# Sparse attention on two sequences in turns, with transfers that serve both, ahead of a routed expert layer

## The chip, the cores and the metric

The kernel runs on one core of a Trainium2 chip. The metric is the device time of one execution in microseconds (us); a kernel's time is the median of its runs. All arithmetic that matters here is float32.

## What is computed

The reference has two stages. The first is block-sparse attention over 4 sequences of 768 tokens, with 8 heads of 64 channels. A sequence has 24 blocks of 32 tokens. A query block sees its own block, its two neighbours, the first and the last block, and three random blocks that the input `sampled_blocks` names; the first and the last query block see all keys. The second stage sends each token to one of 8 experts, by the cosine of its attention output with 8 embeddings, and puts it through that expert's two matrices.

```python
scores = scale * np.matmul(q, k.transpose(0, 1, 3, 2))
mask = np.abs(blk_i - blk_j) <= window
mask = mask | (blk_i == 0) | (blk_j == 0) | (blk_i == n_blocks - 1) | (blk_j == n_blocks - 1)
# ... and True for the three sampled blocks of each query block
attn = softmax(np.where(mask, scores, -1e9))
x = np.matmul(attn, v)                        # (4, 8, 768, 64) -> 3072 tokens of 512
...
expert_idx = argmax(cosine(x, expert_emb) / tau)
out[mask_e] = gate * (np.maximum(x[mask_e] @ w1[e], 0.0) @ w2[e])
```

## The kernel before, in words

**Steps.** A sequence is cut into 6 chunks of 128 queries, rotated by one block, so that chunk 0 holds the last block, the first block and blocks 1 and 2. The loop of `attention_fast` (L1272) makes one chunk per step, s = 0 to 23, and a last step 24 that finishes chunk 23: sequence 0's six chunks, then sequence 1's, and so on. Step s scores chunk s and weighs the values of chunk s-1. In the order of the program a step does:

- `fetch_all` (L434): the loads of this step and the gathers for chunk s+1, all issued from the SyncE queue (SP);
- `score_near` (L510, tile `ac`) and `score_far` (L541, `dps`): scores with near keys and with gathered keys, each followed by an exponential on ScalarE;
- `gather_k` (L484): copies of key blocks for chunk s+1, by VectorE and GpSimd;
- `weigh_near` part 0, `turn_x` of chunk s-2 (L677), one `turn_k` (L456), `weigh_far` (L627): PE's products with V;
- `near_v` (L445): four GpSimd copies of neighbour blocks of V into the gather tile of chunk s+1;
- `turn_q` of chunk s+1 (L472), the logits of chunk s-2, `weigh_near` part 1, `normalize` (L645).

`manual_schedule` keeps the attention in this order on each engine; behind it a scheduler interleaves the experts.

**Queries that see all keys.** In the step that scores a sequence's chunk 0, `score_ends` (L561, tile `bps`) makes the scores of the first and last query block with all 768 keys, four head pairs into four tiles `pb`; the next step's `weigh_far` multiplies them with all six V tiles (L638). For that all of a sequence's K and V must be there at its first chunk.

**V.** `load_v` brings a whole sequence into one of two tiles `vst` (8 DMAs). `gather_v` (L424) fetches, for each of 4 query blocks and 3 random slots, a block of 32 tokens x 8 heads straight from DRAM into a gather tile `vg`, at an offset in a register: 12 DMAs of 64 KB per chunk (6 for chunk 0), into a ring of 3 tiles. `fetch_all` puts the step's other loads between them: K of the next sequence, Q of chunk s+3, V of the next sequence. A row of Q, K or V is 64 float32 values, 256 bytes, and each is a packet of its own.

**The start.** SP issues in order the K of sequence 0 (8 DMAs), the embeddings and tau (`load_experts`, L201), the V of sequence 0 (8), and then, once the offsets are known, the gathers. ScalarE's queue issues the Q of chunks 0 and 1. PE turns the four K pairs and makes `score_ends` between them. `build_experts` (L209) normalizes the embeddings, in pieces put between the first steps.

**Routing.** `after_sequence` (L1193) plans `route` (L740) of a whole sequence of 6 chunks over the steps behind it: a power on GpSimd, some ten small VectorE operations, the one-hot choice, running counts (`seen`, L773) on GpSimd, and x written to DRAM. After two sequences `dispatch_early` assigns tokens to 5 early expert tiles; two `fetch_rows` (L1037) and the first expert's weights (8 DMAs of 512 KB) follow from step 20 on. The last sequence's `route` runs between the first expert tiles (`last_route`, L1437), ahead of `rank` (L800).

**The experts.** 25 tiles of up to 128 tokens follow, some 14 us each: two matrix products per tile (L1126, L1139), with 4 MB of weights each.

Of the kernel before, what the change touches and what calls it, by code (L numbers as in the profile page):

```python
# [12 lines left out]
F32 = mybir.dt.float32  # L13
# [39 lines left out]
NCH = B * NC  # L53
DEN_LOW, DEN_HIGH = 0.1, 1e10
# [72 lines left out]
def build_tokens(k, shifted):  # L127
# [3 lines left out]
    nc.gpsimd.iota(tok, pattern=[[-S, B], [-P, NC]], base=N + BLK * shifted, channel_multiplier=-1)  # L131
    if shifted:
        first = tok.rearrange("p (b c) -> p b c", c=NC)[:, :, 0]
        nc.vector.tensor_scalar(out=first[0:BLK], in0=first[0:BLK], scalar1=-S, scalar2=None, op0=ALU.add)
# [245 lines left out]
def load_q(k, n):  # L380

    b, c = divmod(n, NC)
    k.raw["q", n] = t = k.ld.tile([P, H, D], F32, name="qraw", tag="qraw", bufs=3)
    src = k.q[b].rearrange("h s d -> s h d")
    return [(t[rows], src[lo:lo + rows.stop - rows.start]) for rows, lo in pieces(c)]


def load_k(k, g, pool=None):

    b, j = divmod(g, NPAIR)  # L390
    k.raw["k", g] = t = (pool or k.ld).tile([P, NC, 2, D], F32, name="kraw", tag="kraw", bufs=2 if pool else 3)
# [3 lines left out]
def load_v(k, b):  # L395

    v = k.vst[b % 2]
    src = k.v[b].rearrange("h s d -> s h d")
    parts = []
    parts.append((v[0:BLK, 0, :, 0:D], src[S - BLK:S]))  # L400
    parts.append((v[BLK:P, 0, :, 0:D], src[0:P - BLK]))
    for m in range(1, NC):
        parts.append((v[:, m, :, 0:D], src[P * m - BLK:P * (m + 1) - BLK]))
    return parts


def keep_ends(k, b):

    k.nc.gpsimd.tensor_copy(out=k.vg0[b % 2][D:P], in_=k.vst[b % 2][0:D, 0])
# [14 lines left out]
def gather_v(k, n):  # L424

    b, c = divmod(n, NC)
    k.vg[n] = t = k.vg_ring[n % len(k.vg_ring)]
    src = k.v[b].rearrange("h s d -> s h d")
    for s in range(NRAND):
        for g, shift in zip(blocks_of(c), shifts(k, mybir.EngineType.SP, s, c)):  # L430
            yield t[s * BLK:(s + 1) * BLK, g, :, 0:D], src[bass.ds(shift, BLK)]
# [13 lines left out]
def near_v(k, n):  # L445

    b, c = divmod(n, NC)
    for g in blocks_of(c):
        block = NG * c + g - 2 if g % 2 == 0 else NG * c + g
        if 0 < block < NB - 1:  # L450
            rows, m = home(block)
            k.nc.gpsimd.tensor_copy(out=k.vg[n][NRAND * BLK:P, g], in_=k.vst[b % 2][rows, m])  # L452


def turn_k(k, g):

    nc = k.nc
    b, j = divmod(g, NPAIR)
    raw = k.raw.pop(("k", g))
# [4 lines left out]
    copy(out=k.kt[b % 2][:, j].rearrange("p (w t) -> p w t", w=2), in_=ps[:, :, 0:3 * P])  # L464
    pairs = slice(j, j + 1) if b == 0 else slice(0, NPAIR)
    if j == pairs.stop - 1:
        for i, block in enumerate((NB - 1, 0)):
            nc.scalar.copy(out=k.ke[b % 2][:, pairs, i * BLK:(i + 1) * BLK],
                           in_=k.kt[b % 2][:, pairs, block * BLK:(block + 1) * BLK])


def turn_q(k, n):  # L472

    raw = k.raw.pop(("q", n))
    ps = ring(k, "xg_ps", 0, 1, k.eps, [P, ND, P])
    for j in range(NPAIR):
        k.nc.tensor.transpose(ps[:, j], raw[:, 2 * j:2 * j + 2, :].rearrange("p h d -> p (h d)"), k.ident)  # L477
# [6 lines left out]
def gather_k(k, n):  # L484

    nc = k.nc
    b, c = divmod(n, NC)
    kt = k.kt[b % 2]
# [21 lines left out]
def score_near(k, n):  # L510

    nc = k.nc
    b, c = divmod(n, NC)
    kt, qt = k.kt[b % 2], k.qt[n]
    ps = k.big.tile([P, 2, 512], F32, name="ac", tag="big")
    halves = (1,) if c == 0 else (0, 1)
    for j in range(NPAIR):
        for half in (None, *halves):
            r, lo = near_at(j, half)
            for h in range(2):  # L520
                rows = slice(D * h, D * (h + 1))
                if half is None:
                    cols = slice(D * halves[0], P)
                    keys = k.ke[b % 2][rows, j]
# [15 lines left out]
def score_far(k, n):  # L540

    nc = k.nc
    b, c = divmod(n, NC)
# [17 lines left out]
def score_ends(k, n, j):  # L561

    nc = k.nc
    b = n // NC
    kt, qt = k.kt[b % 2], k.qt[n]
    ps = k.big.tile([P, 2, 512], F32, name="bps", tag="big")
    for m in range(NC):
        for r in range(2):
            for h in range(2):
                rows = slice(D * h, D * (h + 1))  # L570
                lo = D * (2 * m + r) - BLK
                keys = k.ke[b % 2][rows, j] if m == 0 and r == 0 else kt[rows, j, lo:lo + D]
                nc.tensor.matmul(ps[D * r:D * (r + 1), h, D * m:D * (m + 1)], lhsT=keys, rhs=qt[rows, j, h, 0:D],  # L573
                                 start=True, stop=True)
    k.pb[j] = e = k.pb_pool.tile([P, 2, NC, D], F32, name=f"pb{j}", tag=f"pb{j}")
    nc.scalar.activation(e.rearrange("p h m t -> p h (m t)"), ps[:, :, 0:NC * D], ACT.Exp, scale=SCALE)

# [17 lines left out]
def weigh_near(k, n, turn):  # L595

    b, c = divmod(n, NC)
# [955 lines left out]
```

## Time and profile before

| | |
|---|---|
| median of 3 runs | 655.94 us (649.62 to 663.33) |
| the profiled execution: its time, its span | 656.3 us, 654.5 us |
| mean granted TensorE clock | 0.970 |
| PE, weight loads (PEld) busy | 609.0 us (93%), 476.1 us (73%) |
| VectorE (DVE), GpSimd (POOL), ScalarE (ACT) busy | 226.1, 235.2, 118.8 us |
| attention | from 0 to 287.5 us |
| expert tiles | from 277 us on; alone from 301 us on |

All times below that begin at 0 count from the start of the span. The profile is one execution, with the instructions of each engine, the DMA packets and the semaphores. The chain of waits follows the work that ended last back to the start: each piece is the instruction that ran, or the DMA that was waited for. The table of windows gives for chosen stretches the length, then each engine's busy time (with its instructions), PE's granted clock, the mean busy share of the 16 DMA engines, and the GB/s that they moved. SPq is SP's queue, where DMAs are issued; an issue that is long is not a transfer that is long.

### The profile page before, as it was taken

What the parts mean: (1) busy time and instruction counts of PE and PEld (TensorE: products, weight loads), DVE (VectorE), ACT (ScalarE), POOL (GpSimd) and SP (SyncE); (2) the same over time, 40 slices, a digit from 0 to 9 for tenths busy, and PEclk for the clock granted to TensorE, in tenths of its full rate; (3) what the DMA queues carried; (4) which work ended last, traced back from release to release, by engine and by line L of the source; (5) the groups of instructions that cost most, each with busy time, mean ns of one, the idle gap of its engine ahead of it and who ended that gap; (6) DMA issues with size and microseconds to landing.
All of it is one profiled execution on the core that took longest, in us unless ns stands there. A gap on an engine that the chain in (4) does not pass through costs nothing.

```text
span 654.5 us, 21692 instructions
## 1 busy us (share of the span) xinstructions
PE 609.0 (93%) x9016; PEld 476.1 (73%) x9016; DVE 226.1 (35%) x661; ACT 118.8 (18%) x265; POOL 235.2 (36%) x446
## 2 busy tenths in 40 slices
PE   7799899896989799797999999999999999999995
PEld 5598789886989699676776677774667756666773
DVE  6654436542656556127511121122112111211210
ACT  2424344343243324100000000000000000000000
POOL 1853252534163428002033334443333443333332
PEclk9999999899998989797999999999999999999999
DMA  9866666768576757999999989999899998999611
GB/s 189 165 150 146 145 150 137 160 141 212 131 160 140 193 125 190 198 322 397 368 406 394 393 338 307 340 349 340 310 401 402 403 375 307 416 388 404 265 49 33
DMA packets 189758, 170.80 MB, mean 261 GB/s; under 512 B 150152, under 2 KB 150280, under 8 KB 186834
## 3 DMA queue, kind: packets, MB, share of 16 engines
q1 hardware_dynamic: 182338, 155.36, 75.3%
q0 software_dynamic: 5216, 13.43, 6.0%
q8 instruction: 73, 1.20, 0.8%
q10 hardware_dynamic: 2096, 0.52, 0.4%
q14 instruction: 35, 0.29, 0.1%
HBM read 156.65 MB, written 12.90 MB: 259 GB/s over the span
## 4 chain that ended last, share of the span: by engine, by line
PE 83%; issue 4%; DMA 3%; POOL 2%; DVE 2%; SPq 2%; ACT 1%; POOLq 0%; DVEq 0%; ACTq 0%
PE hp L1126 26%; PE yp L1139 24%; PE av L586 11%; PE dps L551 5%; PE ac L529 3%; PE yp L693 3%; DMA vg<-in_v_dram 2%; PE hp L1171 2%; PE yp L1191 2%; PE xg_ps L682 2%; PE xg_ps L477 2%; PE bps L573 2%; SPq L440 1%; PE kps L462 1%; DMA vst<-in_v_dram 1%
## 5 line engine op out<-in xcount | busy, mean ns | idle before, releaser
L1126 PEld LDWEIGHTS hp<-xgt,w 128*128 128x128 f32 x1472 | 170.5, 195 | 10.2 <-issue 10.2
L1126 PE MATMUL hp<-xgt,w 128*128 128x128 f32 x1472 | 171.4, 278 | 0.0
L1139 PE MATMUL yp<-w,h 128*128 128x512 f32 x368 | 162.0, 593 | 0.0
L1139 PEld LDWEIGHTS yp<-w,h 128*128 128x128 f32 x368 | 68.2, 190 | 76.5 <-issue 76.2
L1050 POOL DMA_INDIRECT xg<-x_dram,quarter x88 | 88.5, 1006 | 30.1 <-issue 27.4
L1152 POOL DMA_INDIRECT out_dram<-y,slot_l x20 | 20.3, 1015 | 156.8 <-DVE y L1151 156.8
L494 POOL COPY kg<-kt 128x128 f32 x176 | 44.6, 297 | 65.4 <-issue 36.6
L1129 ACT ACTIVATE h<-hp 128x512 f32<-128x512 f32 x23 | 13.7, 597 | 290.8 <-PE hp L1126 290.8
L452 POOL COPY vg<-vst 32x520 f32<-32x520 f32 x80 | 49.7, 621 | 39.8 <-PE av L586 28.0
L1133 DVE TENSOR_SCALAR h<-hp 128x512 f32<-128x512 f32 x23 | 15.9, 691 | 134.8 <-PE hp L1126 134.8
L586 PE MATMUL av<-vst,pac 64*64 64x65 f32 x1056 | 49.1, 231 | 7.1 <-issue 6.2
L481 DVE COPY qt<-xg_ps 64x512 f32<-64x512 f32 x48 | 33.0, 688 | 57.8 <-PE xg_ps L477 57.1
L1151 DVE TENSOR_SCALAR y<-yp,gate 128x512 f32<-128x512 f32 x20 | 15.0, 751 | 102.3 <-PE yp L1139 90.1
L551 PE MATMUL dps<-qt,kg 128*64 128x64 f32 x1408 | 47.9, 226 | 2.0 <-issue 2.0
L551 PEld LDWEIGHTS dps<-qt,kg 128*64 128x64 f32 x1408 | 44.4, 141 | 3.9 <-issue 2.3
L586 PEld LDWEIGHTS av<-vst,pac 64*64 64x64 f32 x1056 | 40.8, 142 | 6.5 <-issue 3.6
L586 PE MATMUL av<-vg,pd 128*32 128x65 f32 x1408 | 31.4, 230 | 10.9 <-DMA vg<-in_v_dram 4.4
L586 PEld LDWEIGHTS av<-vg,pd 128*32 128x32 f32 x1408 | 25.4, 115 | 17.0 <-issue 9.8
L556 ACT ACTIVATE pd<-dps,bias 128x256 f32<-128x256 f32 x88 | 34.6, 473 | 6.8 <-PE dps L551 6.2
L684 DVE COPY xt<-xg_ps 128x512 f32<-128x512 f32 x24 | 16.5, 688 | 46.3 <-PE xg_ps L682 46.3
L529 PE MATMUL ac<-qt,ke 64*64 64x128 f32 (+1 forms) x384 | 28.8, 276 | 1.3 <-DVE qt L481 1.3
L586 PE MATMUL av<-vg,pac 64*64 64x65 f32 x352 | 29.4, 240 | 0.5 <-issue 0.5
(229 smaller groups left out, 629.7 us busy)
## 6 DMA issues: line engine op xcount, KB each, us to landing
w<-in_moe_w_dram SPq DMA_DIRECT2D x52, 2048.0 KB, 17.1
vg<-in_v_dram SPq DMA_DIRECT2D x264, 64.0 KB, 3.2
kraw<-in_k_dram SPq DMA_DIRECT2D x32, 192.0 KB, 3.4
vst<-in_v_dram SPq DMA_DIRECT2D x20, 256.0 KB, 5.3
qraw<-in_q_dram SPq DMA_DIRECT2D x19, 256.0 KB, 4.3
w<-in_moe_w_dram SPq DMA_DIRECT2D x8, 512.0 KB, 5.8
x_dram<-x SPq DMA_DIRECT2D x4, 774.0 KB, 6.7
x_dram<-x SPq DMA_DIRECT2D x4, 516.0 KB, 3.4
```

Source lines behind the costliest of these rows:

```text
L452: k.nc.gpsimd.tensor_copy(out=k.vg[n][NRAND * BLK:P, g], in_=k.vst[b % 2][rows, m])
L481: k.nc.vector.tensor_copy(out=t[rows, :, h], in_=ps[rows])
L494: copy(out=t[:, :, g, s * BLK:(s + 1) * BLK], in_=kt[:, :, bass.ds(shift, BLK)])
L529: nc.tensor.matmul(ps[D * r:D * (r + 1), h, lo:lo + cols.stop - cols.start], lhsT=keys, rhs=qt[rows, j, h, cols], start=True, stop=True)
L551: nc.tensor.matmul(out[D * r:D * (r + 1), NG * j + g], lhsT=kg[:, j, g, D * r:D * (r + 1)], rhs=qt[:, j, :, cols], start=True, stop=True)
L556: nc.scalar.activation(e[:, :, g].rearrange("p j h t -> p j (h t)"), out.rearrange("p (j g) h t -> p j g (h t)", g=NG)[:, :, g], ACT.Exp, ...
L586: k.nc.tensor.matmul(av[lanes, h // NPAIR, h % NPAIR * P:h % NPAIR * P + D + 1], lhsT=lhsT, rhs=rhs, start=first[0], stop=last, skip_group ...
L693: k.nc.tensor.matmul(ps[:, 0:E], lhsT=xt[:, j], rhs=k.en[:, j, :], start=(j == 0), stop=(j == ND - 1))
L1050: k.nc.gpsimd.indirect_dma_start(out=x[:, g], out_offset=None, in_=quarters, in_offset=bass.IndirectOffsetOnAxis(ap=k.quarter[:, g, t:t + ...
L1126: nc.tensor.matmul(hp[:, f, :], lhsT=w1[:, d, (f0 + f) * P:(f0 + f + 1) * P], rhs=xt[:, d, :], start=(d == 0), stop=(d == ND - 1))
L1139: nc.tensor.matmul(yp, lhsT=h[:, f, :], rhs=w2[:, f, :], start=(f == 0), stop=(f == NF - 1))
L1152: k.scattered = nc.gpsimd.indirect_dma_start(out=k.out[:, :], out_offset=bass.IndirectOffsetOnAxis(ap=slot, axis=0), in_=y[:, :], in_offse ...
```

## The change

The steps now alternate between two sequences: step n is chunk c of sequence DUO*a + i, with i = n mod 2. Steps 0 to 11 are the chunks of sequences 0 and 1, steps 12 to 23 those of 2 and 3.

- One DMA brings Q rows, V rows or a random V block of both sequences: 16 rows of 256 bytes per token instead of 8. A gather is issued for a pair of steps, at the even one, behind `weigh_far` and `turn_q` of that step; the gather ring has 2 tiles of twice the size, the ring of Q tiles 2 of twice the size in place of 3.
- V lies in 7 tiles, one per chunk position, each for both sequences; the second pair's tile m takes the place of tile m-1. `near_v` copies both sequences in one copy, two of the four groups per step.
- K of sequences 2 and 3 is loaded and turned at listed steps (`loading`, `turning`); K of 0 and 1 is loaded at the start, and sequence 1's is turned in step 0.
- `score_ends` moves from the step that scores a chunk 0 to the next one, two head pairs at a time, through two `pb` tiles instead of four.
- `route` runs for 2 chunks, 12 times instead of 4; x goes out in one DMA (two for chunk 0) where a sequence took four. `rank` still runs per 6 chunks.
- `load_experts` stands behind the 16 K loads and the first V tile. `fetch_rows` of tile 1 moves from step 20 to the end of the attention.

```diff
+DUO = 2
+NS = NCH // DUO
+NV = NC + 1
...
+def place(n):
+
+    a, rest = divmod(n, DUO * NC)
+    c, i = divmod(rest, DUO)
+    return DUO * a + i, c, i
...
+def both(src, a):
+
+    return src[DUO * a:DUO * (a + 1)].rearrange("i h s d -> s (i h) d")
+
+
+def load_q(k, s):
+
+    a, c = divmod(s, NC)
+    k.raw["q", s] = t = k.ld.tile([P, DUO * H, D], F32, name="qraw", tag="qraw", bufs=2)
+    src = both(k.q, a)
...
+def gather_v(k, s):
+
+    a, c = divmod(s, NC)
+    k.vg[s] = t = k.vg_ring[s % len(k.vg_ring)]
+    src = both(k.v, a)
+    for r in range(NRAND):
+        for g, shift in zip(blocks_of(c), shifts(k, mybir.EngineType.SP, r, c)):
+            yield (t[r * BLK:(r + 1) * BLK, g].rearrange("p i h e -> p (i h) e")[:, :, 0:D], src[bass.ds(shift, BLK)])
...
+def near_v(k, s, some):
+
+    a, c = divmod(s, NC)
     for g in blocks_of(c):
         block = NG * c + g - 2 if g % 2 == 0 else NG * c + g
-        if 0 < block < NB - 1:
+        if g in some and 0 < block < NB - 1:
             rows, m = home(block)
-            k.nc.gpsimd.tensor_copy(out=k.vg[n][NRAND * BLK:P, g], in_=k.vst[b % 2][rows, m])
+            k.nc.gpsimd.tensor_copy(out=k.vg_ring[s % len(k.vg_ring)][NRAND * BLK:P, g], in_=vtile(k, a, m)[rows])
...
+    n.vg_ring = [n.gp.tile([P, NG, DUO, H, D + 1], F32, name=f"vg{i}", tag=f"vg{i}", bufs=1) for i in range(2)]
...
+    for s in range(2):
+        for to, src in load_q(n, s):
+            nc.scalar.dma_start(out=to, in_=src)
+    for g in range(2 * NPAIR):
+        fetch_all(n, None, load_k(n, g, n.setup if g < 5 else None))
+    fetch_all(n, None, load_v(n, 0, 0))
     load_experts(n)
-    fetch_all(n, None, load_v(n, 0))
...
+    fetch_all(n, 0, [])
+    for m in range(1, NC):
+        fetch_all(n, None, load_v(n, 0, m))
     turn_q(n, 0)
     for g in range(NPAIR):
         turn_k(n, g)
-        if g:
-            score_ends(n, 0, g - 1)
-    score_ends(n, 0, NPAIR - 1)
...
+    turning = {0: range(NPAIR, 2 * NPAIR), 3: (8,), 5: (9,), 7: (10,), 9: (11,), 10: (12, 13), 11: (14, 15)}
+    loading = {1: (8,), 3: (9,), 5: (10,), 7: (11, 12), 9: (13, 14), 10: (15,)}
...
+        if s == 0:
+            for g in turning[0]:
+                turn_k(n, g)
...
+        if ends:
+            score_ends(n, s - 1, 0)
+            score_ends(n, s - 1, 2)
         if s >= 2:
             turn_x(n, s - 2)
...
         if s >= 1:
             weigh_far(n, s - 1)
+        if ends:
+            weigh_ends(n, s - 1, (0, 2))
+            score_ends(n, s - 1, 1)
+            score_ends(n, s - 1, 3)
         if s + 1 < NCH:
-            near_v(n, s + 1)
             turn_q(n, s + 1)
         if s >= 2:
             chunk_logits(n, s - 2)
+        ahead, odd = s // DUO + 1, s % DUO
+        loads = []
+        if odd and ahead - 1 < NC:
+            loads += load_v(n, 1, ahead - 1)
+        for g in loading.get(s, ()):
+            loads += load_k(n, g)
+        if not odd and ahead + 1 < NS:
+            loads += load_q(n, ahead + 1)
+        if ahead < NS:
+            if not odd:
+                fetch_all(n, ahead, loads)
+                near_v(n, ahead, (0, 1))
+            else:
+                fetch_all(n, None, loads)
+                near_v(n, ahead, (2, 3))
...
+        if ends:
+            weigh_ends(n, s - 1, (1, 3))
         if s >= 1:
             weigh_near(n, s - 1, 1)
             normalize(n, s - 1)
...
-                for _ in route(n, B - 1):
+                for _ in route(n, NS - 1):
                     pass
 
+        fetch_rows(n, 1)
         expert_tiles(n, between(), partial(turn_x, n, NCH - 1), last_route, last_rank, lambda: next(n.late))
```

## The prediction

> **What bounds the kernel now.** I sum against the profiled execution, 656.3 us (span 654.5, so 1.8 us lie around it); the median of three runs is 655.94, so the two stand for each other. I read the page's slices first, then the windows, then SP's timeline, then the chain. The slices say that PE is above 90% from the sixteenth on (the experts, alone from 301 us, which the change leaves alone) and at 60 to 90% before. So the attention decides. Its steps, cut at each step's first `ac` on PE (column two is the length):
>
> ```profile
> 37.90:78.10 40.20, 35.94 (x1041) 32.53 (x1040) 19.03 (x57) 15.46 (x36) 14.84 (x42) 1.00 0.72 155
> 78.10:140.00 61.90, 57.84 (x1744) 53.82 (x1740) 30.79 (x97) 24.84 (x57) 26.24 (x75) 0.94 0.67 147
> 101.90:119.10 17.20, 17.20 (x533) 16.14 (x530) 11.96 (x42) 7.56 (x18) 7.31 (x24) 1.00 0.65 145
> 140.00:208.10 68.10, 60.47 (x1748) 55.75 (x1745) 32.00 (x104) 24.96 (x57) 27.17 (x77) 0.92 0.70 161
> 208.10:274.50 66.40, 57.56 (x1739) 52.71 (x1734) 35.33 (x125) 22.89 (x53) 27.23 (x64) 0.94 0.77 175
> 235.60:258.80 23.20, 23.20 (x767) 21.64 (x767) 17.30 (x60) 10.23 (x25) 15.76 (x40) 1.00 0.64 162
> ```
>
> In two windows PE is full at clock 1.00. They give the clean price of a step: 8.60 us with a `turn_k` (17.20 over two), 7.73 without (23.20 over three), so 0.87 per `turn_k`. The pair of steps around a sequence's first chunk is clean at 21.9 (PE's busy time in such steps where the clock was 1.00, one `turn_k` within). Clean, steps 2 to 5 with three `turn_k` would take 4 x 7.73 + 3 x 0.87 = 33.5 us, the next two sixes 21.9 + 33.5 = 55.4 each, the last six, without a `turn_k`, 51.9: 196.2 in all. Steps 2 to 23 take 40.2 + 61.9 + 68.1 + 66.4 = 236.6. So 40.4 us go to waits, and to clock stretches at half speed. What are the waits for?
>
> ```profile
> 106.69 0.82 SPq L440 DMA_DIRECT2D vg<-in_v_dram  x2
> 107.98 0.32 SPq L438 DMA_DIRECT2D vst<-in_v_dram  x1
> 108.51 2.87 SPq L440 DMA_DIRECT2D vg<-in_v_dram  x4
> 111.48 0.40 SPq L438 DMA_DIRECT2D kraw<-in_k_dram  x1
> ```
>
> SP issues without a pause, even where PE is full. From 37.9 to 258.8 us its records add to 182.0 us, gaps under 0.15 us to 34.5, and real waiting to 4.2 of 220.9. That is 216.5 us for 299 DMAs, 0.72 each with the register work and the long issues:
>
> ```profile
> L440 SPq DMA_DIRECT2D vg<-in_v_dram x264: 316/317/2007, 19.1 to 276.8; - x132
> ```
>
> The median issue takes 0.317 us and the longest 2.0. Per two steps SP needs 216.5 / 11 = 19.7 us, PE 15.5 to 17.2. So SP's queue paces the steps. The chain where PE waits has SP's issues right ahead of the landing:
>
> ```profile
> 133.35 1.39 SPq L440
> 134.79 0.05 SPq L440
> 134.94 2.05 DMA vg<-in_v_dram
> 137.12 1.07 PE av L586 x57
> ```
>
> Later two stretches wait for the transfers themselves, behind the first weights, and the end waits for GpSimd's running counts ahead of `rank`:
>
> ```profile
> 257.29 5.79 DMA vg<-in_v_dram
> 263.62 5.20 DMA vg<-in_v_dram
> 301.07 0.21 POOL seen L773
> 301.32 0.20 PE rk L802
> ```
>
> **Part 1: fewer issues.** From step 2 on SP issues 120 gathers (10 pairs of 12) instead of twice as many, 7 V, 9 Q, 16 K, 12 x and 3 weight DMAs: 167. At 0.72 each that is 120 us, 11.0 per pair of steps. What a 128-KB gather (512 rows of 256 bytes) costs SP, no row shows. Below: 0.32 us, a median gather of 256 rows. Above: double, 1.45 with its share of long issues, were it by rows. I take today's 0.72, since V loads of 1,024 rows issue in 0.40 and are nearest in kind. So PE (some 16.5 per pair), not SP, paces. SP paces again from 0.72 + (16.5 - 11.0) x 11/120 = 1.2 us on. What is late next is PE itself, where it is not data.
>
> **Part 2: the new waits.** A pair's gathers wait, in the even step, for `weigh_far` of the step before (ring of 2), and the Q load for `turn_q`. Everything behind them on SP waits too: V, K, x. They are needed at `weigh_far` three steps on, some 24 us; 12 issues at 0.72 and a landing of 6.2 (the longest seen at 64 KB) take 15. Ten us are left, and cover it.
>
> **Part 3: the transfers.** Bytes and 256-byte packets stay. Steps 2 to 11 need about 17.6 MB (10.6 of gathers, V, Q, K and x) in 90 us, 196 GB/s, where 145 to 175 ran. The bound from below is the start, when the queue was full:
>
> ```profile
> 4.00:12.00 8.00, 6.18 (x40) 3.86 (x42) 6.20 (x8) 0.79 (x3) 0.40 (x3) 1.00 1.11 246
> 12.00:20.00 8.00, 6.41 (x218) 5.47 (x212) 5.12 (x25) 4.55 (x12) 2.33 (x6) 1.00 1.18 205
> ```
>
> So 205 to 246 GB/s can be had, 4 to 25% above need; I add 3 us in these pairs. A gain is not excluded below: the two waits of 5.79 and 5.20 go, as the last gathers are issued before weights. The clean sum already leaves them out.
>
> **Part 4: the later start.** Today step 2 begins at 37.9. After, 16 K loads (3.15 MB), Q (1.05), V of both sequences (3.15) and six gathers (0.79) stand ahead of the end of the last V tile, itself counted: 8.1 MB. At 246 GB/s it lands at 37 (issues begin at 4), at 205 at 43.5; I take 40. `weigh_ends` of step 1 needs every V tile. The rest of step 1 (`score_ends` 2.6, `weigh_ends` 3.6, `turn_q`, `weigh_near`, by their rows) is 9 to 10 us, so step 2 begins at 50 (46 to 56): +12.1. The embeddings, now behind K and V, land at about 22, and ScalarE's `emb_sq` stands in its queue before the exponentials of step 0; GpSimd's `near_v` waits for V tile 1 and holds `gather_k` of step 1. Both end before the 40 us, so that I price them at nothing; were the V early, they would show.
>
> **Part 5: PE work.** `score_ends` and `weigh_ends` only move. Three more `turn_k` lie before step 2: -2.6. First-chunk steps now have two `pb` tiles, so PE waits for exponentials (0.81 us each in the rows of `pb`) that other heads cover; with the near-first order I allow 4 us over four such steps, bounds 0 and 7. One half-clock stretch more or less is 1.7 us; I add one.
>
> **Part 6: routes.** Twelve instead of four: each has some ten VectorE operations (2.1 us) and 2.7 us of GpSimd with its power. Per step that adds 0.7 to VectorE (of 17.30/3 = 5.8 now) and 0.9 to GpSimd (15.76/3 = 5.3), so 6.5 and 6.2 of 7.7. A `near_v` copy of twice the size (0.62 us now) is at most 1.24, with half as many. They stay beside PE's work; if that cover goes, each us over 7.7 is a us of the step. At the end `seen` has 2 additions instead of 6, and `rank` of the last sequence stands later, within tile 1's products: -3 of the 3.57 us wait (0 to 3.57).
>
> **Sum.** Steps 2 to 23: 196.2 - 2.6 + 3 (transfers) + 4 (`pb`) + 1.7 (clock) + 0.8 for the rows of tile 1, now fetched only at the end, = 203.1, against 236.6: -33.5. Start +12.1, end -3. 656.3 - 24.4 = 632 us.
>
> [...] The issue queue is full for 216.5 of 220.9 us, though the median issue, 0.317 us, is short beside the landing (3.2). [...] The sum goes by the row of 1,024-row loads at 0.40 us.
>
> **The rivals.**
> - R1, *issue by rows*: a gather costs SP 1.45 us. Then 11.0 + 0.72 x 120/11 = 18.9 per pair; the ten ordinary pairs take 189 instead of 163: +26, in place of the 9 us of stalls, so 649. For: long issues (48 over 0.6 us) are most of the 0.72. Against: 0.40 for four times the rows. It decides from 1.2 us per gather.
> - R2, *other side: the transfers pace already*. If 256-byte packets move at the 145 to 161 GB/s of today's steps whatever is queued, the same bytes take the same 236.6 us: 656.3 + 12.1 - 3 = 665, slower. For: DMA share 0.65 to 0.77 in the steps. Against: 246 GB/s in the start, share 1.11. It decides when steps 2 to 23 shrink by less than the 9.1 us that start and end cost: a rate under 236.6/227.5 of today's (about 160), 166 GB/s. Halfway, at 175 to 180 in steps 2 to 11, it costs some 10 us: 642.
> - R3, *the start costs more*: V at 50, because the queue's order delays it or `emb_sq` and `near_v` chain up: step 2 at 60, 642.
> - R4, *VectorE or GpSimd become the bound*: a route's chain lengthens each of 22 steps by 0.8 us: +17, 649. For: GpSimd's `near_v` and `gather_k` stand in line with `pow` (1.49). Against: 1.2 to 1.5 us free in each step.
>
> **How the numbers follow.** The forecast 0.55; R1 0.11; R2 full 0.08, halfway 0.09; R3 0.08; R4 0.09. The likeliest one's own range, from step 2 at 46 or 56 and the stalls' bounds, is 619 to 644. A low end of 614 takes the stalls at nothing and the start at 46 with a clock like today's; a high end of 655 takes in R1, R3, R4 and the halfway R2, and leaves R2 out. A measurement of this kernel tells about 2% (13 us) from no change: faster means under 642.8, slower over 669. Faster: 0.54 of the forecast, about half of halfway R2 and R3 (0.09), some of R1 and R4 (0.04): 0.67. Slower: most of R2's upper tail and sums of R3 with R1 or R4: 0.07. Same: 0.26.
>
> **What the profile after would show.** Right: SP's queue with pauses in the steps; 132 gathers at a median issue near 0.35 us; windows of steps with PE full and DMA share near 0.8; step 2 at about 50; the attention's end near 264 (287.5 - 24); under 1 us ahead of `rank`. R1: gathers over 1.2 us, SP without pauses. R2: PE waiting for `vg` with DMA share near 1. R3: step 2 at 60. R4: PE waiting for `kg`, `qt` or `x` copies. The forecast is wrong if steps still take 10 us.

## The result and the profile after

The changed kernel takes 671.01 us (median of 4 runs, 670.08 to 673.24) beside 653.5 us for the kernel before (median of 4, 649.62 to 663.33): a ratio of 1.029 with a 95% interval of 1.022 to 1.037. The ratio is of the fast runs and leaves out the slow one of before, 663.33 us. It is slower; 632 us was forecast. The profiled executions, 654.5 and 671.5 us of span, differ by 17.0 us, and three milestones say where. The forecast column splits the prediction's sum at the same milestones.

| | before, us | changed, us | difference | forecast |
|---|---|---|---|---|
| step 2 begins | 37.9 | 60.7 | +22.8 | +12.1 |
| steps 2 to 22 | 220.9 | 230.3 | +9.4 | -26.3 |
| step 23 to the second expert tile's first product | 42.8 | 30.4 | -12.4 | -10.2 |
| the rest | 352.9 | 350.1 | -2.8 | 0 |

The page first: as many products, half as many gathers, the same bytes (170.77 MB in all beside 170.80), and the share of SP's queue, q1, up from 75.3%.

```profile
PE 606.3 (90%) x9016; PEld 472.5 (70%) x9016; DVE 230.7 (34%) x739; ACT 119.6 (18%) x267; POOL 239.1 (36%) x450
q1 hardware_dynamic: 177698, 154.82, 82.2%
q8 instruction: 73, 1.20, 0.8%
vg<-in_v_dram SPq DMA_DIRECT2D x132, 128.0 KB, 5.2
```

The windows of the changed kernel's start (columns as before: stretch and length, busy time of PE, PEld, DVE, ACT and POOL with instructions, PE's clock, DMA share, GB/s):

```profile
4.00:12.00 8.00, 3.90 (x14) 2.23 (x12) 1.67 (x5) 1.49 (x2) 0.00 (x0) 0.86 1.32 192
12.00:20.00 8.00, 4.37 (x19) 3.25 (x18) 3.19 (x8) 1.00 (x2) 0.00 (x0) 0.72 1.23 216
20.00:30.00 10.00, 2.32 (x64) 2.02 (x64) 2.24 (x18) 2.70 (x8) 1.52 (x5) 0.84 1.22 185
30.00:40.00 10.00, 6.93 (x70) 5.89 (x72) 4.52 (x11) 4.35 (x10) 5.15 (x10) 0.82 1.20 203
40.00:50.00 10.00, 6.09 (x173) 5.49 (x171) 5.41 (x20) 2.53 (x5) 9.55 (x29) 0.69 1.32 198
50.00:60.70 10.70, 8.26 (x210) 7.51 (x210) 1.55 (x3) 1.62 (x2) 1.81 (x2) 0.82 1.22 162
```

With both sequences' K, Q and V to bring, the transfers keep the DMA engines full (a share of 1.2 or more) from 4 us to step 2, at 162 to 216 GB/s, where the same 4 to 12 us of before moved 246. PE is busy for 31.9 of these 56.7 us, and its clock falls to 0.69.

All of steps 2 to 22, first of the kernel before, then of the changed one, and three stretches of the latter in which twelve gathers are issued; last, a stretch without transfers:

```profile
37.90:258.80 220.90, 200.42 (x5987) 185.04 (x5987) 114.06 (x373) 84.78 (x195) 94.04 (x255) 0.95 0.68 156
60.70:291.00 230.30, 199.80 (x6022) 183.92 (x6023) 120.41 (x439) 84.25 (x197) 93.88 (x252) 0.95 0.87 153
72.60:84.60 12.00, 12.00 (x380) 11.36 (x381) 7.51 (x22) 3.43 (x9) 2.78 (x9) 1.00 0.88 162
94.70:105.40 10.70, 10.32 (x264) 9.66 (x263) 4.59 (x19) 4.28 (x10) 8.21 (x26) 0.82 1.27 167
115.10:126.80 11.70, 10.95 (x344) 10.10 (x344) 8.99 (x30) 4.34 (x12) 10.89 (x28) 1.00 1.08 154
63.00:72.00 9.00, 8.51 (x339) 7.84 (x333) 1.87 (x9) 5.80 (x11) 4.05 (x10) 1.00 0.01 4
```

PE's busy time is that of before (199.8 us beside 200.4); its idle time rose from 20.5 to 30.5 us, and that is the 9.4 us. The mean rate, 153 GB/s, is that of before (156), but it comes in bursts of 154 to 167 GB/s at a share of 0.88 to 1.27, with pauses between. SP's timeline shows both:

```profile
72.00 0.37 SPq L459 DMA_DIRECT2D qraw<-in_q_dram  x1
72.55 12.01 SPq L461 DMA_DIRECT2D vg<-in_v_dram  x12
84.67 0.43 SPq L463 DMA_DIRECT2D vt<-in_v_dram  x1
85.15 4.38 SPq L463 DMA_DIRECT2D kraw<-in_k_dram  x2
94.11 0.37 SPq L459 DMA_DIRECT2D qraw<-in_q_dram  x1
```

Twelve gathers take 12 us, two K loads 4.4 (one K issue was 0.45 us in the steps before), and then SP has nothing to do until 94. Over steps 2 to 22 SP's longer pauses (over 0.15 us, between its first and its last instruction there) add to 60.9 us (4.2 before). SP no longer paces, as forecast; PE did not get faster for it. What PE waits for in these steps (us in total, times, longest):

```profile
PEld av L619 <- issue: 16.0, 30, 2.9
PE av L619 <- issue: 9.4, 9, 2.8
PE kps L484 <- DMA kraw<-in_k_dram: 5.6, 1, 5.6
PE xg_ps L499 <- DVE xt L713: 2.1, 1, 2.1
```

"issue" is time in which PE waited for nothing that the profile shows (PE's and PEld's rows overlap). One such gap in PE's timeline is this:

```profile
92.16 0.87 PE L619 MATMUL av<-vg,pd 128*32 128x65 f32 x21 [2.60 <-issue]
```

The DMA packets of the trace name the cause. Queue q8 carries 73 packets of 16,384 bytes; PE runs 18,032 products and weight loads, 247 for each packet. A packet of q8 lands at 90.86, and PE goes on at 92.16, 1.30 us later. So it is with gap after gap: of PE's idle time in steps 2 to 22, 20.8 us in 24 gaps end 1.2 to 1.8 us behind such a packet. The same reading of the trace of before gives 15.0 of 20.4 us. The gaps that the profile explains otherwise are the control: in steps 2 to 22 of the twenty kernels profiled for this document, 362 of the 373 gaps over 0.15 us marked "issue" end 1.1 to 1.8 us behind a packet of q8, and 12 of the 173 gaps for which the profile names a releaser do. PE waits for its own instructions. How far ahead PE fetches them, no run here shows.

### The profile page after: what moved, and what is told of

Same layout as the page of the kernel before. It is cut to its first block, busy times and chain, and to the rows that moved or that the text cites. A ratio compares the mean times of both kernels' runs of the same rounds, so it can differ in the third digit from the quotient of the medians.

```text
span 671.5 us, 21249 instructions
## 1 busy us (share of the span) xinstructions
PE 606.3 (90%) x9016; PEld 472.5 (70%) x9016; DVE 230.7 (34%) x739; ACT 119.6 (18%) x267; POOL 239.1 (36%) x450
## 2 busy tenths in 40 slices
DMA packets 187164, 170.77 MB, mean 254 GB/s; under 512 B 147560, under 2 KB 147688, under 8 KB 184242
## 4 chain that ended last, share of the span: by engine, by line
PE 81%; SPq 6%; issue 5%; DMA 3%; DVE 2%; ACT 1%; POOL 1%; POOLq 0%; DVEq 0%; ACTq 0%
PE hp L1154 25%; PE yp L1167 24%; PE av L619 11%; PE dps L573 4%; SPq L463 4%; PE yp L722 3%; PE ac L551 3%; PE hp L1199 2%; PE yp L1219 2%; PE bps L595 2%; PE xg_ps L499 2%; SPq L461 2%; DMA vt<-in_v_dram 2%; PE xg_ps L711 2%; DMA vg<-in_v_dram 1%
## 5 line engine op out<-in xcount | busy, mean ns | idle before, releaser
L1154 PEld LDWEIGHTS hp<-xgt,w 128*128 128x128 f32 x1472 | 167.8, 192 | 10.3 <-issue 10.2
L1154 PE MATMUL hp<-xgt,w 128*128 128x128 f32 x1472 | 169.3, 275 | 0.0
L1180 POOL DMA_INDIRECT out_dram<-y,slot_l x20 | 20.5, 1025 | 155.9 <-DVE y L1179 155.9
L473 POOL COPY vg<-vt 32x1040 f32<-32x1040 f32 x40 | 42.1, 1053 | 59.7 <-PE av L619 53.2
L619 PE MATMUL av<-vt,pac 64*64 64x65 f32 x704 | 46.5, 226 | 0.9 <-DVE x L811 0.7
L619 PE MATMUL av<-vg,pac 64*64 64x65 f32 x704 | 38.3, 234 | 4.1 <-issue 4.1
L619 PEld LDWEIGHTS av<-vt,pac 64*64 64x64 f32 x704 | 38.4, 140 | 3.1 <-issue 1.4
L619 PE MATMUL av<-vg,pd 128*32 128x65 f32 x1408 | 30.0, 233 | 7.4 <-issue 5.9
L619 PEld LDWEIGHTS av<-vg,pac 64*64 64x64 f32 x704 | 30.2, 138 | 5.3 <-issue 4.7
L619 PEld LDWEIGHTS av<-vg,pd 128*32 128x32 f32 x1408 | 24.4, 116 | 12.9 <-issue 12.1
```

What stands on the lines that cost most here:

```text
L473: k.nc.gpsimd.tensor_copy(out=k.vg_ring[s % len(k.vg_ring)][NRAND * BLK:P, g], in_=vtile(k, a, m)[rows])
L619: k.nc.tensor.matmul(av[lanes, h // NPAIR, h % NPAIR * P:h % NPAIR * P + D + 1], lhsT=lhsT, rhs=rhs, start=first[0], stop=last, skip_group ...
L1154: nc.tensor.matmul(hp[:, f, :], lhsT=w1[:, d, (f0 + f) * P:(f0 + f + 1) * P], rhs=xt[:, d, :], start=(d == 0), stop=(d == ND - 1))
L1180: k.scattered = nc.gpsimd.indirect_dma_start(out=k.out[:, :], out_offset=bass.IndirectOffsetOnAxis(ap=slot, axis=0), in_=y[:, :], in_offse ...
```

## The experiments

Kernels that leave gathers out or bring other values deal the tokens to the experts otherwise, so their total times are not compared; their steps are (b_half_rows, with as many products as before, is the exception). "Instructions": PE's idle time that ends behind a packet of q8. "Other": the rest of PE's idle time. "Lost to clock": half of the time that the records show at half clock, whether PE was busy or not. "SP": SP's longer pauses. All but the first and last column are for steps 2 to 22, in us, of one profiled execution. Seven kernels with the changed kernel's traffic in the steps (the changed one, a_emb, a_start, a_spread, a_warm, a_k_once, w_even) lie between 228.6 and 233.0: so well does one execution repeat. Each ratio is to runs of the kernel before taken beside it, whose medians were 653.5 to 660.5 us.

| kernel | step 2 at | steps | instructions | other | lost to clock | SP | time (ratio to before) |
|---|---|---|---|---|---|---|---|
| before | 37.9 | 220.9 | 15.0 | 5.4 | 10.2 | 4.2 | 653.5 |
| changed | 60.7 | 230.3 | 20.8 | 9.4 | 12.1 | 60.9 | 671.0 (1.029) |
| b_half_rows | 36.2 | 221.0 | 14.4 | 7.5 | 6.8 | 5.6 | 652.1 (0.988, 0.976 to 1.001) |
| b_half_dmas | 37.3 | 209.1 | 13.1 | 1.8 | 2.3 | 59.1 | |
| b_no_gathers | 36.9 | 202.5 | 10.6 | 0.2 | 5.1 | 148 | |
| a_half_rows | 55.6 | 212.0 | 11.3 | 7.2 | 3.4 | 69.9 | |
| a_no_gathers | 57.6 | 206.1 | 6.6 | 6.5 | 6.8 | 141 | |
| a_two_64 | 59.5 | 232.6 | 4.5 | 29.9 | 17.1 | 22.1 | 688.8 (1.048) |
| a_emb | 59.3 | 228.6 | 24.1 | 6.0 | 7.3 | 69.6 | 673.7 (1.039) |
| a_start | 59.9 | 230.7 | 24.1 | 5.1 | 12.1 | 72.5 | 672.0 (1.035) |
| a_warm | 56.6 | 231.1 | 27.7 | 7.0 | 5.1 | 67.3 | 671.2 (1.019) |
| a_k_once | 52.2 | 233.0 | 21.2 | 6.3 | 16.2 | 73.1 | 672.1, one run |
| a_spread | 60.3 | 232.2 | 23.9 | 10.7 | 8.5 | 66.3 | 674.9 (1.039) |
| w_even | 57.6 | 230.8 | 26.6 | 4.9 | 8.5 | 63.7 | 676.0 (1.029) |
| w_pace | 56.2 | 229.1 | 21.3 | 11.9 | 8.5 | 52.0 | 675.5 (1.038) |
| b_act_kq | 36.3 | 263.3 | 4.8 | 36.1 | 30.7 | 85.8 | 695.9 (1.058) |
| a_act_kq | 57.4 | 243.9 | 21.3 | 13.9 | 18.8 | 121 | 685.6 (1.040) |
| a_two_64_act | 64.5 | 261.0 | 5.7 | 36.3 | 39.3 | 88.5 | 719.6 (1.091) |
| a_fixed_32 | 59.9 | 227.8 | 23.9 | 7.0 | 6.8 | 68.7 | |
| a_fixed_96 | 56.9 | 220.6 | 14.6 | 6.8 | 8.5 | 61.6 | |

**What paced the kernel before.** Half of the heads of each gather, in `gather_v`:

```diff
-            yield t[s * BLK:(s + 1) * BLK, g, :, 0:D], src[bass.ds(shift, BLK)]
+            yield t[s * BLK:(s + 1) * BLK, g, 0:H // 2, 0:D], src[bass.ds(shift, BLK), 0:H // 2]
```

> The kernel before, with as many gathers (264), each bringing 4 of the 8 heads only (128 packets of 256 bytes instead of 256, 32 KB); the other heads' rows of the gather tile stay zero, so that part of the attention is left out. Theory 'issue' (the prediction's: SP's time per DMA paces the steps): the number of DMAs is the same, steps 2 to 23 stay within 5 us of 236.6, the time within 648 to 660. Theory 'transfers' (the DMA engines' time for 256-byte packets paces, a long issue is the queue pushing back, and PE's own instruction packets of queue q8 come late for the same reason): 17.3 MB of gathers become 8.7; PE's 24 us of idle time in the steps and most of the 12 us lost to the clock go: steps near 200 to 210, the time 620 to 632.

Every second gather (b_half_dmas), and all but chunk 0's (b_no_gathers):

```diff
+            if g % 2 == 0:       # b_half_dmas
+            if n == 0:           # b_no_gathers
                 yield t[s * BLK:(s + 1) * BLK, g, :, 0:D], src[bass.ds(shift, BLK)]
```

> The kernel before with every second gather left out (132 of 64 KB; half of the random blocks are not brought, their rows stay zero). 'Issue': SP needs 132 x 0.72 = 95 us less, PE alone is left: 620 to 632. 'Transfers': the same bytes as with half of the heads, so the same time within 6 us of that run. Only the pair of runs tells: equal and fast is 'transfers', this one fast and the other near 655 is 'issue'.

> The kernel before with the gathers of chunk 0 of the first sequence alone (6 of 264): the random blocks of V are left out. It asks what PE's waits for its own instruction packets (queue q8; 15.0 us in steps 2 to 22 of before, 14.4 with half of the bytes, 13.1 with half of the DMAs) hang on. If on the transfers beside them: under 4 us, steps 2 to 22 at 190 to 196. If on PE's stream of small matmuls alone: 10 to 15 us again, steps at 203 to 209. Experts are dealt other tokens here, so only the steps are compared.

Steps 2 to 22 of the two halves, b_half_rows first, then of b_no_gathers (columns as above):

```profile
36.20:257.20 221.00, 198.60 (x5987) 182.60 (x5987) 112.47 (x373) 85.04 (x195) 97.37 (x258) 0.97 0.54 127
```

```profile
37.30:246.40 209.10, 194.00 (x5986) 178.47 (x5985) 114.30 (x373) 84.97 (x195) 95.76 (x256) 0.99 0.63 148
```

```profile
36.90:239.40 202.50, 191.61 (x5985) 178.32 (x5984) 113.23 (x373) 85.16 (x195) 94.34 (x254) 0.97 0.41 102
```

Half of the bytes with all issues: 221.0, nothing gained, and SP as full as ever (pauses of 5.6 us). Half of the issues: 209.1. So "issue" is right, SP paced the kernel before; the time of b_half_rows agrees (0.988, not clear of 1). But halving the gathers is worth 11.8 us, not the 23 to 35 that the expectation had, and leaving them all out 18.4. Of the waits for instructions 13.1 us stay, and 10.6 without the gathers: PE's stream of small products meets them without that traffic, though not without any, for the other loads still move 102 GB/s. That is the floor that the prediction did not know: 202.5, not 188.5 (its clean 196.2 less step 23's 7.7).

**Traffic in the changed kernel.** One sequence's rows only (a_half_rows), all but the first pair's gathers (a_no_gathers); both zero the gather tiles first:

```diff
+            if s == 0:           # a_no_gathers
                 yield (t[r * BLK:(r + 1) * BLK, g].rearrange("p i h e -> p (i h) e")[:, :, 0:D], src[bass.ds(shift, BLK)])
-  ...[:, :, 0:D], src[bass.ds(shift, BLK)])
+  ...[:, 0:H, 0:D], src[bass.ds(shift, BLK), 0:H])      # a_half_rows
```

> The changed kernel with 132 gathers of one sequence's heads only (256 packets, 64 KB, the DMA's size of before); the other sequence's rows stay zero, so that part is left out; the gather tiles are zeroed first. 'Transfers': half of the gathered bytes, PE's waits for instruction packets (20.8 us in the steps) shrink to under 8, steps 2 to 23 fall from 242 to 205 to 215, the start stays (step 2 near 58): 635 to 648. 'Waits' (what the change lost is SP's waiting for turn_q and weigh_far, 78 us of pauses, which bytes do not alter): steps stay above 230, the time 660 to 672.

> The changed kernel with the gathers of the first pair of chunks alone (6 of 132): the random blocks of V are left out, the gather tiles zeroed first. The floor of the changed order of work. 'Transfers' (what the change lost in the steps comes from the traffic of the gathers): steps 2 to 22 at 200 to 206 as with no gathers in the kernel before (202.6), instruction waits 8 to 12 us. 'Order' (the moved score_ends, 12 routes, two pb tiles cost it): steps above 212.

Steps 2 to 22 of a_half_rows, then of a_no_gathers:

```profile
55.60:267.60 212.00, 193.06 (x6022) 178.25 (x6022) 120.51 (x439) 83.75 (x197) 93.58 (x252) 0.98 0.59 135
```

```profile
57.60:263.70 206.10, 192.89 (x6020) 179.23 (x6020) 121.80 (x439) 84.08 (x197) 93.50 (x252) 0.97 0.39 98
```

All bytes 230.3, half 212.0, none 206.1; the waits for instructions go 20.8, 11.3, 6.6 (under 8 were expected of the half). The moved work, the 12 routes and the two `pb` tiles cost 206.1 - 202.5 = 3.6 us, or 6.2 with the three `turn_k` that now lie ahead of step 2; the gathers' traffic costs 24, now that SP is not the brake. "Transfers" holds for the changed kernel, as "issue" did for the one before. Of the 24 us, 14.2 are waits for instructions, 2.9 other idle time and 6.9 busy time, half of it clock (its loss while PE is busy falls from 10.2 to 6.8).

Each gather as two DMAs of 64 KB (a_two_64) undoes the doubling alone:

```diff
+            for lo in (0, H):
+                yield (t[...][:, lo:lo + H, 0:D], src[bass.ds(shift, BLK), lo:lo + H])
```

> The changed kernel with each 128-KB gather split into two DMAs of 64 KB, one per sequence: the doubling alone undone, same bytes, same waits, 264 gathers. 'Transfers': the count of DMAs does not matter, 668 to 676. 'Issue': SP's work rises by 132 DMAs at 0.3 to 0.7 us, 40 to 90 us over the steps; with SP's 78 us of pauses partly taking it, 675 to 700.

The time, 688.8, falls where "issue" put it, and the reason is a wait that neither theory named. PE's waits in it:

```profile
PE kps L486 <- DMA kraw<-in_k_dram: 25.2, 4, 12.9
```

K stands behind the gathers on SP, whose pauses are down to 22.1 us, and comes late four times. Waits for instructions are 4.5 us; whether smaller transfers spare them, or PE's standing still for K hides them, this run does not tell.

**The start.** The embeddings behind the first sequence's K (a_emb); further V tiles 0 and 1 and the first gathers ahead of the second sequence's K (a_start):

```diff
-    for g in range(2 * NPAIR):
-        fetch_all(n, None, load_k(n, g, n.setup if g < 5 else None))
-    fetch_all(n, None, load_v(n, 0, 0))
-    load_experts(n)
+    for g in range(NPAIR):
+        fetch_all(n, None, load_k(n, g, n.setup))
+    load_experts(n)
+    for m in range(2):
+        fetch_all(n, None, load_v(n, 0, m))
...
     fetch_all(n, 0, [])
-    for m in range(1, NC):
+    for g in range(NPAIR, 2 * NPAIR):
+        fetch_all(n, None, load_k(n, g, n.setup if g < 5 else None))
+    for m in range(2, NC):
         fetch_all(n, None, load_v(n, 0, m))
```

> The changed kernel with the embeddings and tau loaded behind the K of the first sequence, not behind all K and V tile 0. Theory 'queue order of ScalarE' (PE's 6.5 us at 23.9 wait for exponentials behind emb_sq): that wait goes, but the chain behind V tile 1 (near_v, then the embeddings' last steps on VectorE, PE's 3.9 us at 41.7) stays: step 2 at 54 to 59, the time 664 to 670. Theory 'bytes' (the start is set by V's last tile): step 2 stays within 2 us of 60.7, no change.

> The changed kernel with SP's first loads in the order K of sequence 0, embeddings, V tiles 0 and 1, gathers, K of sequence 1, V tiles 2 to 5. 'Queue order': both waits go, PE is not idle long enough for half a clock, and V's last tile (about 45) and 9 to 10 us behind it are left: step 2 at 50 to 54 as the prediction had it, the time 659 to 665. 'Bytes': step 2 stays near 60.

Both come out as "bytes" said, the time too. PE's wait of 6.5 us behind `emb_sq` goes in a_emb, step 1 begins at 30.2 instead of 37.2, and step 2 still at 59.3. In a_start PE's clock averages 0.63 from 21 to 60 us, so that step 1's work takes 20 us. Two more kernels part clock from bytes. a_warm puts dummy products of zeros ahead of the first eight `turn_k` and of step 1; a_k_once loads one sequence's K only and turns it twice:

```diff
+            warm_up(n, 5)
             turn_k(n, g)
...
-        fetch_all(n, None, load_k(n, g, n.setup if g < 5 else None))
+        n.raw["k", g] = n.raw["k", g - NPAIR]      # a_k_once, for the second sequence
```

> The changed kernel with the start reordered as before (embeddings, V tiles 0 and 1 ahead of the second sequence's K), which left step 2 at 59.9 with PE's clock at 0.50 from 12 to 30 and from 40 to 50, and now with dummy products of zeros ahead of each of the first eight turn_k (4 and 5 of 0.6 us) and ahead of step 1. 'Clock' (PE, idle for data, runs the work of step 1 at half speed): the clock stays near 1.00, step 1 takes 12 to 14 us instead of 20, step 2 at 51 to 55, the time 662 to 667. 'Bytes' (V's last tile sets the start whatever the clock): step 2 stays within 2 us of 60.

> The changed kernel with the K of the second sequence not loaded at the start (the first sequence's tiles are turned a second time; that sequence's scores are wrong): 1.57 of the 8.1 MB ahead of V's last tile go. 'Bytes' (the start is as long as its loads): V's last tile lands 8 us earlier and step 2 begins at 51 to 54 instead of 60.7. 'PE' (the order of work and the half clock): 58 to 61.

From 40 to 50 us of a_start, then of a_warm:

```profile
40.00:50.00 10.00, 9.61 (x212) 8.58 (x210) 7.22 (x24) 3.70 (x7) 9.55 (x29) 0.50 1.37 201
```

```profile
40.00:50.00 10.00, 6.71 (x225) 5.77 (x225) 8.85 (x28) 3.94 (x9) 9.49 (x29) 1.00 1.04 197
```

With the clock at 1.00 from 40 us on, a_warm's step 2 begins at 56.6: 3.3 us under a_start, less than "clock" expected. With 1.57 MB less, a_k_once's begins at 52.2, 8.5 us earlier, which is 185 GB/s: "bytes". (Eight DMAs go with the bytes; that the engines' share was 1.17 or more in every stretch speaks for the bytes.) Both parts are shown, bytes the larger. Neither shortens the whole: 671.2, and 672.1 in one run. In a_warm the waits for instructions rise to 27.7 us.

**When the transfers run.** Six gathers per step instead of twelve in the even one, loads between them (a_spread); the same with a_warm's start and each K a step or two earlier (w_even); the same with a 4-byte transfer behind each gather (w_pace):

```diff
-                fetch_all(n, ahead, loads)
+                n.some = gather_v(n, ahead)
+                fetch_some(n, loads)               # 6 of n.some, a load ahead of each two
...
-    loading = {1: (8,), 3: (9,), 5: (10,), 7: (11, 12), 9: (13, 14), 10: (15,)}
+    loading = {1: (8,), 3: (9,), 5: (10,), 6: (11,), 7: (12,), 8: (13,), 9: (14,), 10: (15,)}
...
+        k.nc.sync.dma_start(out=k.bit[0:1, k.bits % 16:k.bits % 16 + 1], in_=k.q[0, 0, 0:1, 0:1])
```

> The changed kernel with six of a pair's gathers issued in the even step and six in the odd one, the loads of K and V between them, instead of twelve in a row ahead of K and V. 'Bursts' (twelve 128-KB gathers in a row delay K, 5.5 us at 150.6, and PE's instruction packets, 20.8 us in steps 2 to 22): K's wait goes, the instruction waits shrink to 10 to 15, steps 2 to 22 fall from 230 to 212 to 220, the time 655 to 664. 'Bytes alone': steps within 4 us of 230, the time 668 to 674.

> The changed kernel with the reordered and warmed start of the run before (step 2 at 56.6, steps 2 to 22 at 231.1, instruction waits 27.7 us), six gathers per step, and each K one step or two earlier. 'K late': the 5 us wait at 149 goes, steps at 222 to 227, the time 664 to 668. Engines' queues stay full as often (share of 1 or more ahead of half of PE's instruction packets), so the instruction waits stay at 20 to 28 us.

> The same with a transfer of 4 bytes behind each gather: of the eight transfers that may be under way four are then gathers, half as many bytes wait in the engines' queues, and SP needs some 0.4 us more per gather (19 us per pair of steps, as before the change). 'Backlog' (an instruction packet waits behind the bytes queued ahead of it): fewer packets meet a share of 1, instruction waits 8 to 15 us, steps 2 to 22 at 210 to 218, the time 650 to 660. 'Bytes alone': the waits stay above 20 us, steps at 222 to 235, the time 664 to 678.

Steps 2 to 22 of w_even, then of w_pace:

```profile
57.60:288.40 230.80, 199.20 (x6019) 182.67 (x6017) 119.95 (x439) 84.30 (x197) 94.10 (x252) 0.96 0.91 148
```

```profile
56.20:285.30 229.10, 195.80 (x6019) 179.68 (x6018) 119.92 (x439) 83.84 (x197) 93.61 (x252) 0.96 0.74 150
```

All three leave the steps at 229 to 232. w_even loses the wait for K, as expected, and has it back in waits for instructions (26.6), so that its steps miss the 222 to 227 that followed from K alone. w_pace lowers the mean DMA share from 0.91 to 0.74 and the waits only to 21.3, while `turn_k` waits again (10.3 us). "Bytes alone" it is: neither the bursts nor the depth of what is queued explains the 24 us, at least in these forms.

**Another queue.** The loads of K and Q inside the steps issued by ScalarE, in the kernel before (b_act_kq), the changed one (a_act_kq) and a_two_64 (a_two_64_act):

```diff
-        k.nc.sync.dma_start(out=to, in_=src)
+        (k.nc.scalar if raw and k.act else k.nc.sync).dma_start(out=to, in_=src)
```

> The kernel before with the loads of K and Q inside the steps issued from ScalarE's queue instead of SP's: 42 of SP's 299 DMAs in the steps go, with the same bytes and the same gathers. 'Issue' (SP paces the kernel before): SP is freed of 42 x 0.72 = 30 us, more than the 12 us that halving the gathers brought, so steps 2 to 22 fall from 220.9 to 209 to 214, the time 7 to 12 us under before. 'Not SP': the steps stay within 3 us, the time within 5 us of before.

> The changed kernel with the loads of K and Q inside the steps issued from ScalarE's queue. 'Bursts' (K waits behind twelve gathers): K's 5.5 us at 150.6 goes, steps 2 to 22 at 222 to 226; PE's instruction waits of 20.8 us stay, since the transfers stay; the time 663 to 668. 'Bytes alone': steps within 3 us of 230, 669 to 674.

> The changed kernel with 64-KB gathers (two DMAs per block) and K and Q issued from ScalarE's queue. With 64-KB gathers alone PE's instruction waits were 4.5 us instead of 20.8, but K came 25 us too late. 'Size of a transfer' (a 128-KB gather ahead of it delays an instruction packet more than a 64-KB one): instruction waits under 11 us without K's waits, steps 2 to 22 at 208 to 217, the time 650 to 660. 'Hidden by K's waits' (PE's instructions came early only because PE stood still for K): instruction waits 13 to 20 us again, steps above 222, 662 to 672.

All three are much slower and miss the times that either of their theories expected, for a reason outside of the question. What SP waits for in b_act_kq:

```profile
SPq L445 <- DMA kraw<-in_k_dram: 39.7, 12, 5.5
SPq L445 <- DMA qraw<-in_q_dram: 39.1, 16, 4.5
```

A gather on SP now waits until a K or Q load that ScalarE issued has landed: at 140.5 SP stops ahead of a gather, ScalarE gets to its Q load at 140.81, behind its own work, and SP goes on at 145.03. The gather does not read that load; the program gives the transfers of both queues the same eight semaphores in turn (this gather waits for the one that the Q load holds, which lands at 145.01). So these runs are inconclusive on SP's pace and on the size of a transfer, and they price the move itself: +42 us in the steps of before, +14 in those of the changed kernel.

**The form of a gather.** Fixed blocks in place of the sampled ones, into 32 partitions as before (a_fixed_32) or the same stretch into 96 (a_fixed_96):

```diff
+            yield (t[r * BLK:(r + 1) * BLK, g]...[:, :, 0:D], src[D * c + BLK * r:D * c + BLK * (r + 1)])
+            yield (t[0:NRAND * BLK, g]...[:, 5 * r:5 * r + 5, 0:D], src[D * c:D * c + NRAND * BLK, 5 * r:5 * r + 5])
```

> The changed kernel with gathers of the same form (32 partitions x 16 rows of 256 bytes, 132 of 128 KB) from fixed blocks of V instead of the sampled ones (no register reads; other values are weighed). The control of the next run: steps 2 to 22 at 224 to 234, instruction waits 17 to 26 us, if the random addresses and their registers cost nothing of note.

> The same with each gather spread over 96 partitions x 5 rows (480 packets of 256 bytes instead of 512, 6 per cent fewer bytes, the same fixed stretch of V; other values are weighed). The prediction took its rate for gathers (205 to 246 GB/s) from K and V loads, which write 128 partitions. 'Form' (a gather into 32 partitions drains slower than a load into 96 or more): the twelve gathers of a pair are issued in 7 to 9 us instead of 11 to 12, steps at 210 to 220, waits for instructions 10 to 16 us. 'Bytes alone': both within 5 us of each other.

SP's timeline of a_fixed_32, then of a_fixed_96:

```profile
93.27 11.93 SPq L462 DMA_DIRECT2D vg<-in_v_dram  x12
113.60 11.85 SPq L462 DMA_DIRECT2D vg<-in_v_dram  x12
```

```profile
90.86 8.95 SPq L462 DMA_DIRECT2D vg<-in_v_dram  x12
108.51 10.15 SPq L462 DMA_DIRECT2D vg<-in_v_dram  x12
```

Without any register work twelve gathers still take SP 11.9 us (10.2 to 12.4 over the steps), so the register work is not what takes the time: 12 x 131 KB in 11.9 us are 132 GB/s. That the transfers hold the issue up fits this, but only in part: with half of the bytes per gather (a_half_rows) twelve still take SP 8.2 to 10.0 us. Into 96 partitions they take 9 to 10 us (145 to 165 GB/s), the steps 220.6 instead of 227.8, the waits 14.6 instead of 23.9. 6% of fewer bytes is worth 0.06 x 24 = 1.4 us of the 7.2. So form counts, but for less than half of the 24 us; neither theory came out as written, since "form" had 210 to 220 for the steps and "bytes alone" a difference under 5.

## Why the prediction was wrong

Two steps failed. The larger is part 3, which put the transfers at 3 us; the other is the clean price, which put PE's waits for its own instructions at nothing. Steps 2 to 22 were forecast at 194.6 us and took 230.3, 35.7 more: 21.2 of it is the gathers' traffic (24.2 measured, 3 put in), and 14.5 the floor without it (206.1 measured in a_no_gathers, 191.6 forecast). The late start adds 10.7.

- *What bounds the kernel now: right, and mis-sized.* SP's queue did pace the steps (b_half_rows). But the step "40.4 us go to waits, and to clock stretches" set the whole difference to a clean price against SP. The clean price came from windows without a single gap, the luckiest of the trace. Most of the idle time, 15.0 of 20.4 us, ended behind PE's own instruction packets, which the profile calls "issue" and which the prediction passed over; 10.6 us of it needs no gathers. Worth to be had: 11.8 us by half of the issues. (A slip that changes nothing: 37.9 to 258.8 us are 21 steps, so that SP's 216.5 us are 20.6 per pair of steps, not 19.7.)
- *Part 1 held in what it concluded, not in its price.* A gather's issue takes 0.70 us on average in steps 2 to 22 (median 0.46 over the kernel, 0.35 expected), and 0.93 with its register work and short gaps, which is what the 0.72 had counted. SP needs some 14 us per pair of steps (11.0 taken; K loads rose from 0.6 to 1.5 us each). It still pauses for 60.9 us, and R1 did not come.
- *Part 2 held.* PE waits 1.5 us for a gather in all, in a gap that also ends behind a packet of q8; SP waits 41.6 us for `turn_q` and hides it. The wait that it did not name is K's, behind the gathers: 5.6 us.
- *Part 3 failed most.* 3 us were put in for the transfers; beside a_no_gathers they cost 24. The bounds of 205 to 246 GB/s came from loads of K and V into 128 partitions beside 258 of PE's products in 16 us (some 420 in 16 us of the steps); stretches of twelve gathers moved 154 to 167. R2, with 17% in its two forms, had named the transfers, 166 GB/s as its point of decision, and 665 us, nearest to the 671. But its sign, PE waiting for `vg`, came to 1.5 us: what the traffic holds up is PE's instructions and, once, K.
- *Part 4 was short by 10.7 us.* The rate was 185 to 216 GB/s instead of 246, and V's last tile landed at about 45.8, not 40. And what stood as "price them at nothing", `emb_sq` in ScalarE's queue and `near_v` in GpSimd's, left PE idle for 6.5 and 3.9 us, and 9 to 10 us of work took 15.1 (45.6 to 60.7): 8.3 us of it ran at half clock, and 2.4 went to a gap that ends at 55.8, behind a packet of q8 that lands at 54.3. With a warm clock it took 9.6 (47.0 to 56.6 in a_warm), as forecast. This is R3, which had step 2 at 60 and 8%.
- *Part 5:* clock losses are 12.1 us in steps 2 to 22 (10.2 of it while PE was busy), where 1.7 were added to a clean price; the kernel before lost 10.2 as well, so the clock is no part of the 9.4 us between the two. In both kernels' steps the records show half clock in stretches of 3.41 us or twice that (1.7 us lost per 3.41), behind PE's gaps (the gap of 89.6 to 92.2, half clock from 91.6 to 98.5). So a gap of PE can cost a second time, but few do: these steps have 28 gaps over 0.15 us and five such stretches, each with 0.9 to 2.5 us of idle time in the 3.4 us ahead of it.
- *Part 6 held:* waits for VectorE are 2.1 us, R4 did not come. *The end held:* -12.4 where -10.2 was forecast; `rank` runs at 325.1 without a wait.

The sum for steps 2 to 22, term by term: 185.9 clean as forecast; +20.8 for instructions (0 forecast); +9.4 other idle time (7 forecast for transfers and `pb`); +13.9 by which busy time is longer, 10.2 of it the clock (1.7 forecast): 230.0, and 0.3 in shorter gaps. SP's work in steps 2 to 22 did fall, from 216.7 us to 149.9. Halving the number of DMAs helped, with the same 256-byte packets (b_half_dmas, 209.1 us), and halving the packets per DMA did not (b_half_rows, 221.0). The 0.40 us of the V loads held for V loads (0.43 to 0.66); it said nothing of what the transfers would cost PE.

What stays open: by which path the gathers' traffic delays PE's instruction packets. Pooled over the 941 packets of q8 in steps 2 to 22 of all twenty kernels, the wait behind a packet grows with the DMA engines' share in the 3 us ahead of it:

| share ahead | under 0.25 | to 0.5 | to 0.75 | to 1 | to 1.25 | above |
|---|---|---|---|---|---|---|
| mean wait, us | 0.10 | 0.11 | 0.19 | 0.49 | 0.58 | 0.74 |

Two of 47 packets met a share of 1 or more in the kernel before, 21 of 47 in the changed one. That fits waiting behind queued packets; but w_pace lowered the share and not much of the waits, and in the kernel before 9.8 of the 15.0 us stand behind packets that met a share under 1, so it is argued, not shown. No complete version that was tried beats the kernel before.

## What to carry to other kernels

A full issue queue is worth no more than a run without its work shows: before a gain is put into a sum, take the suspect out (no gathers: 18 us here) rather than compare with the best window of the trace. When a brake is taken off, the rate of the next resource must come from rows of the same form and under the same load, not from the start of the kernel (205 to 246 GB/s there, 154 to 167 while twelve gathers are issued). Work on two sequences at once asks for both sequences' data before the first step is done (step 2 at 60.7 instead of 37.9), and PE, after waiting, worked on at half clock for 8.3 of the last 15 us.

## What the runs showed of the hardware

- PE's small products use up a 16-KB packet of instructions in some 4 us (47 packets in 192 to 200 us of PE's busy time); where PE waited with no releaser named, it went on 1.1 to 1.8 us after such a packet had landed, in 362 of 373 gaps. Without the gathers (98 to 102 GB/s of other traffic) these waits are 6.6 to 10.6 us in 206.1 and 202.5, with them up to 27.7.
- Loads moved to another engine's queue can stop the first queue: 78.8 us of waits on SP for ScalarE's loads in b_act_kq, since this program takes the semaphores of both from the same eight.
- SP's issue of a K load of 192 KB took 0.45 us at the median in the steps of the kernel before, one at a time among gathers, and 0.39 in w_pace; where two or four follow a V load it took 0.92 in the changed kernel and 1.02 without its gathers (a_no_gathers). So the issue of the same load takes two to three times as long in one place as in another.
